# A recurrence and a two-layer network on one core: two transposes by TensorE instead of DMA, in a new order of steps

## The chip, the core and the metric

The kernel runs on one core of a Trainium2 chip. TensorE (PE) multiplies matrices into PSUM; VectorE (DVE), ScalarE (ACT) and GpSimd (POOL) do the element-wise work; SyncE (SP) issues nearly all DMA transfers from one queue. The metric is the device time of one execution in microseconds (us); the figure for a kernel is the median of its runs.

## The reference, cut to what matters

```python
# r, k, v, w: (4 batches, 8 heads, 768 steps, 48); u: (8, 48)
for t in range(768):
    cur = einsum('bhd,bhe->bhde', u * k_t, v_t)
    y[:, :, t] = einsum('bhd,bhde->bhe', r_t, state + cur)
    state = w_t[..., None] * state + einsum('bhd,bhe->bhde', k_t, v_t)
x = y.transpose(0, 2, 1, 3).reshape(3072, 384)
h = x @ w_in                       # (384, 2048)
out = maximum(0.01 * h, h) @ w_out # (2048, 384)
```

The first half is a linear recurrence over time for each batch and head; the second half takes its result y as rows and sends them through two matrix products with a leaky ReLU in between.

## The kernel before, in words

**Tiles.** The 768 steps of a batch are cut into 6 chunks of 128, so there are 24 chunks, numbered 0 to 23 in the order in which they are worked on (the "9th" is chunk 8, the "11th" chunk 10). Chunks 0 to 3 are done in pairs by `pair` (from L537), the others one at a time by `single` (from L741). The network works on blocks of one or two chunks: 15 blocks with 2, 1, 1, 1, 1, 2, 2, 2, 2, 2, 1, 1, 2, 2, 2 chunks.

**One chunk in `single`.** Four DMA loads w, k, r, v, 192 KB each (L755), into one of 10 buffers `in`. ACT takes the logarithm of w (`lw`, L765). PE sums it over time (the step `cum`, L771 and L774), DVE adds `lw` (`ci`, L783), ACT takes exponentials (L797, L801, and the decays `a`, L792), DVE multiplies them with r and k (`rk`, L459). `rk` is transposed to `rkT`, either by PE (L470) with a copy out of PSUM (L475 on DVE, L477 on ACT) or, for the chunks in `RK_DMA`, by a DMA transpose on SP (L818). PE multiplies `rkT` with itself (`scores`, L912, for some pairs of chunks in one step), DVE masks the result (`m`, two operations, L842). `sums` (L852) is the state's new part and DVE adds the old one (L867) that POOL has decayed (`sb`, L829). `intra` (L878 and L883) gives the chunk's product; DVE adds the bonus part to it (`y`, L532), which POOL and DVE prepared (L489, L493, L497, L501).

**From y to the network.** y has to be transposed into `xT`. For a chunk not in `Y_DMA`, `to_xt` does it: three transposes on PE (L518) into the PSUM bank that held the product, then one copy by ACT (L525) or DVE (L523). For a chunk in `Y_DMA`, SP issues one DMA transpose (L897).

**The network.** For each block, `up` steps (L1074) multiply `w_in` with `xT`, ACT applies the leaky ReLU (`g`, L1089), `down` steps (L1104, four for each chunk) multiply `g` with `w_out`; the result is copied out of PSUM (L1115 on DVE, L1117 on ACT) and stored by SP (L1121). The last three blocks of two chunks use a product scheme with seven instead of eight parts (L1006 on PE, with L989, L1020, L1022 and L1027 on DVE and ACT).

**The order.** Nothing runs in the order in which it is written. Each step is entered in a `Plan` with its engines, a duration, a priority and what it depends on. `Plan.order` goes through a list schedule: whenever an engine is free, it takes the ready step with the lowest priority that finds its buffers free. The table `RANK` adds a number to the priority of single steps, and `FORCE` fixes the engine of some that may run on two. The order that comes out is emitted, engine by engine, and on the chip each engine works through its own list strictly in that order, waiting on semaphores. SP's list holds all loads, stores and DMA transposes. There are 8 PSUM banks; at most two are given to `up` results (`hp`) and two to the products of `sums` and `intra` (`yy`).

Of the kernel before, what the change touches and what calls it, by code (L numbers as in the profile page):

```python
# [23 lines left out]
class Plan:  # L24
# [202 lines left out]
FORCE = {23: "DVE", 26: "DVE", 29: "ACT", 30: "DVE", 46: "ACT", 58: "ACT", 61: "ACT", 79: "ACT", 85: "DVE",  # L227
    112: "DVE", 114: "ACT", 117: "DVE", 119: "ACT", 121: "ACT", 123: "DVE", 125: "POOL", 127: "ACT", 128:
    "POOL", 134: "POOL", 137: "DVE", 139: "POOL", 142: "ACT", 143: "POOL", 492: "DVE", 500: "ACT", 604: "DVE",
    612: "ACT", 904: "DVE", 910: "DVE", 932: "ACT", 952: "ACT", 966: "ACT", 1002: "ACT", 1030: "ACT", 1075:  # L230
    "ACT", 1080: "ACT"}


@with_exitstack
def kernel(
# [23 lines left out]
    JQ = NJ // NQ  # L259

    RK_DMA = {6, 11, 12, 14, 15, 16, 17, 18, 19, 20, 21, 22, 23}
    Y_DMA = {8, 10, 16, 17, 20, 21, 22, 23}
    MERGED = {6, 10, 12, 14, 16, 18, 20}
    LEAD = 4
    AHEAD = 4
# [65 lines left out]
    with tc.manual_schedule():  # L331
# [180 lines left out]
        def to_xt(P0, y, yp, s_ye, col_of):  # L512
            def yT():
                return yp.t[:].bitcast(BF16).rearrange("p (g t) -> p g t", t=128)

            def typose(e):
                for g in range(KT):
                    nc.tensor.transpose(  # L518
                        yT()[:, g, :], y.t[:].rearrange("p h d -> p (h d)")[:, g * 128 : (g + 1) * 128], ident[:])

            def xcopy(e):
                if e == "DVE":
                    nc.vector.tensor_copy(out=col_of(), in_=yT()[:, 0:KT, :])  # L523
                else:
                    nc.scalar.copy(out=col_of(), in_=yT()[:, 0:KT, :])  # L525
            s_yt = step({"PE": 0.18}, typose, P0 + 1, deps=[s_ye], reads=[y, yp])
            return step({"ACT": 0.48, "DVE": 0.36}, xcopy, P0 + 1, deps=[s_yt], reads=[yp])
# [213 lines left out]
        def single(n):  # L741
# [149 lines left out]
            col = n * L  # L891
            if n not in Y_DMA:
                xt_steps[n] = [to_xt(P0, y, yp, s_ye, lambda: xT[:, :, col : col + L])]
# [287 lines left out]
```

## Time and profile before

| | |
|---|---|
| median of 3 runs | 180.65 us (180.39 to 180.79) |
| profiled execution | 181.35 us, span 179.6 us |
| granted TensorE clock | 1.000 |
| busy PE / DVE / ACT / POOL | 172.6 / 132.2 / 115.7 / 104.0 us |
| DMA | 34.43 MB in 116715 packets |
| y transposes by DMA (L897) | 8, of 1.23 us on SP (median), 3.5 us to landing |
| y transposes by PE (L518) | 48 matmuls, 219 ns each |

The span runs from the first to the last instruction of the profiled execution; its own time is 1.75 us longer and lies 0.70 us above the median of the runs. A line of a group gives line, engine, operation, out<-in, shapes and count, then busy time and mean duration in ns, then the idle time of the engine just before and what ended it. A line of a stage gives its bounds, its length, then busy time and count for PE, weight loads, DVE, ACT and POOL, the granted clock, the DMA share and GB/s. A line of the timeline or of the chain gives its start and length in us. Matmuls follow one another in a pipeline, so a step's share of PE is read from the start of the next step and not from the duration of its matmuls.

### The profile page before, as it was taken

What the parts mean: (1) busy time and instruction counts of PE and PEld (TensorE: products, weight loads), DVE (VectorE), ACT (ScalarE), POOL (GpSimd) and SP (SyncE); (2) the same over time, 40 slices, a digit from 0 to 9 for tenths busy, and PEclk for the clock granted to TensorE, in tenths of its full rate; (3) what the DMA queues carried; (4) which work ended last, traced back from release to release, by engine and by line L of the source; (5) the groups of instructions that cost most, each with busy time, mean ns of one, the idle gap of its engine ahead of it and who ended that gap; (6) DMA issues with size and microseconds to landing.
All of it is one profiled execution on the core that took longest, in us unless ns stands there. A gap on an engine that the chain in (4) does not pass through costs nothing.

```text
span 179.6 us, 5374 instructions
## 1 busy us (share of the span) xinstructions
PE 172.6 (96%) x2109; PEld 135.2 (75%) x2109; DVE 132.2 (74%) x265; ACT 115.7 (64%) x257; POOL 104.0 (58%) x138
## 2 busy tenths in 40 slices
PE   7998999999999999999999999999999999999991
PEld 2475878867878687787688777677778798899991
DVE  7589974189788898559687659499787599777472
ACT  2568968865957786895379775177675487735620
POOL 5989631675896486878468855414995459200000
PEclk9999999999999999999999999999999999999999
DMA  5999999999999989999899999999599996613004
GB/s 139 261 283 314 370 380 362 176 203 208 215 195 202 192 192 150 183 199 182 193 214 177 218 164 214 212 192 144 117 201 145 198 234 170 153 24 115 0 22 153
DMA packets 116715, 34.43 MB, mean 192 GB/s; under 512 B 109137, under 2 KB 115922, under 8 KB 116690
## 3 DMA queue, kind: packets, MB, share of 16 engines
q1 hardware_dynamic: 116688, 34.09, 90.8%
q8 instruction: 16, 0.26, 0.6%
q14 instruction: 9, 0.07, 0.1%
q10 hardware_dynamic: 2, 0.00, 0.0%
HBM read 25.17 MB, written 4.72 MB: 166 GB/s over the span
## 4 chain that ended last, share of the span: by engine, by line
PE 64%; DVE 8%; DMA 8%; ACT 6%; issue 5%; SPq 4%; POOL 3%; DVEq 0%; ACTq 0%; POOLq 0%
PE ps L1074 26%; PE ps L1104 17%; PE ps L1006 6%; DMA in<-in_w_dram 6%; SPq L755 3%; PE ps L1146 3%; PE ps L912 2%; DMA xT<-y 2%; DVE m L842 2%; POOL ru L489 1%; DVE o L1027 1%; ACT g L1089 1%; PE ps L883 1%; ACT rkT L477 1%; DVE m L690 1%
## 5 line engine op out<-in xcount | busy, mean ns | idle before, releaser
L1074 PE MATMUL ps<-xT,w_in_b 128*128 128x256 bf16 (+1 forms) x720 | 73.1, 251 | 0.4 <-ACT xT L525 0.2
L1089 ACT ACTIVATE g<-ps 128x512 bf16<-128x512 f32 x96 | 56.4, 595 | 20.6 <-PE ps L1074 15.3
L1074 PEld LDWEIGHTS <-w_in_b 128*128 128x128 bf16 x720 | 57.7, 98 | 9.3 <-issue 0.7
L1104 PE MATMUL ps<-w_out_b,g 128*128 128x384 bf16 x288 | 56.0, 326 | 0.1
L1104 PEld LDWEIGHTS <-g 128*128 128x128 bf16 x288 | 25.7, 97 | 12.4 <-ACT g L1089 0.2
L489 POOL TENSOR_TENSOR ru<-in,ub 128x384 f32<-128x384 f32 x24 | 24.5, 1027 | 10.9 <-DMA in<-in_k_dram 10.1
L459 DVE TENSOR_TENSOR rk<-in,ps 128x384 bf16<-128x384 f32 x46 | 24.3, 548 | 7.8 <-ACT ps L797 4.2
L842 DVE TENSOR_TENSOR m<-ps,maskb 128x512 bf16<-128x512 f32 x40 | 25.4, 683 | 6.1 <-PE ps L912 5.0
L493 POOL TENSOR_TENSOR ru<-ru,in 128x384 f32<-128x384 f32 x24 | 24.6, 1030 | 2.9 <-DMA in<-in_r_dram 2.2
L829 POOL TENSOR_TENSOR sb<-s,a 128x384 bf16<-128x384 f32 x18 | 15.7, 873 | 9.5 <-ACT a L792 9.4
L501 POOL TENSOR_TENSOR vs<-in,dg 128x384 f32<-128x384 f32 x20 | 16.6, 828 | 7.1 <-DVE dg L497 4.7
L509 POOL CAST vb<-in 128x384 bf16<-128x384 f32 x24 | 12.0, 503 | 11.3 <-DMA in<-in_v_dram 7.5
L783 DVE TENSOR_TENSOR ci<-ps,lw 128x384 f32<-128x384 f32 x20 | 11.1, 554 | 4.3 <-PE ps L771 1.9
L497 DVE TENSOR_REDUCE dg<-ru 128x8 f32<-128x384 f32 x24 | 12.9, 545 | 1.0 <-POOL ru L493 0.8
L765 ACT ACTIVATE lw<-in 128x384 bf16<-128x384 f32 x20 | 10.4, 520 | 3.6 <-DMA in<-in_w_dram 3.6
L797 ACT ACTIVATE ps<-ps 128x384 f32<-128x384 f32 x20 | 9.5, 475 | 4.2 <-DVE ci L783 3.8
L532 DVE TENSOR_TENSOR y<-ps,vs 128x384 bf16<-128x384 f32 x20 | 11.1, 553 | 1.5 <-PE ps L883 0.6
L867 DVE TENSOR_TENSOR s<-ps,sb 128x384 f32<-128x384 f32 x14 | 7.7, 552 | 4.0 <-PE ps L852 2.8
L801 ACT ACTIVATE ps<-ci 128x384 f32<-128x384 f32 x20 | 9.8, 488 | 0.6 <-DVE ci L783 0.6
L1146 PE MATMUL ps<-zeros 128*128 128x128 bf16 (+1 forms) x40 | 8.7, 339 | 1.3 <-DVE zeros L332 1.3
L525 ACT COPY xT<-ps 128x384 bf16<-128x384 bf16 x11 | 5.2, 481 | 6.8 <-PE ps L518 6.7
L792 ACT ACTIVATE a<-ps 64x4 f32<-64x4 f32 x36 | 6.0, 168 | 5.3 <-DVE ci L783 3.5
(105 smaller groups left out, 228.7 us busy)
## 6 DMA issues: line engine op xcount, KB each, us to landing
out_dram<-o SPq DMA_DIRECT2D x23, 192.0 KB, 3.2
in<-in_w_dram SPq DMA_DIRECT2D x20, 192.0 KB, 4.3
in<-in_k_dram SPq DMA_DIRECT2D x20, 192.0 KB, 4.2
in<-in_r_dram SPq DMA_DIRECT2D x20, 192.0 KB, 4.1
in<-in_v_dram SPq DMA_DIRECT2D x20, 192.0 KB, 4.3
in<-in_moe_w_out_dram SPq DMA_DIRECT2D x4, 768.0 KB, 12.3
in<-in_moe_w_in_dram SPq DMA_DIRECT2D x4, 384.0 KB, 7.0
in<-in_moe_w_in_dram SPq DMA_DIRECT2D x2, 768.0 KB, 9.8
```

Source lines behind the costliest of these rows:

```text
L459: (nc.gpsimd if e == "POOL" else nc.vector).tensor_tensor(out=o, in0=x, in1=i, op=ALU.mult)
L489: lambda e: nc.gpsimd.tensor_tensor(out=ru.t[:], in0=kv(), in1=ubv, op=ALU.mult),
L493: lambda e: nc.gpsimd.tensor_tensor(out=ru.t[:], in0=ru.t[:], in1=rv(), op=ALU.mult),
L497: lambda e: nc.vector.tensor_reduce(out=dg.t[:], in_=ru.t[:], axis=AX.X, op=ALU.add),
L501: lambda e: nc.gpsimd.tensor_tensor(out=vs.t[:], in0=vv(), in1=dg.t[:].unsqueeze(2).to_broadcast([128, H, D]), op=ALU.mult),
L509: {"POOL": 0.56}, lambda e: nc.gpsimd.tensor_copy(out=vb.t[:], in_=vv()),
L829: lambda e: nc.gpsimd.tensor_tensor(out=sb.t[:].rearrange("p g a d -> p (g a) d"), in0=s_in.t[:].rearrange("p g a d -> p (g a) d"), in1=a_ ...
L842: lambda e, par=par: nc.vector.tensor_tensor(out=m.t[:, par, :, :], in0=sc[par].t[:].rearrange("p (g t) -> p g t", g=NP), in1=maskb[:].uns ...
L1074: nc.tensor.matmul(hp.t[:, a * N : (a + 1) * N], lhsT=w_in_b[:, t, (j + a) * 128 : (j + a + 1) * 128], rhs=xT[:, t, c0 : c0 + N], start=(a ...
L1089: lambda e, hp=hp, g=g, j=j, J=J, N=N: nc.scalar.activation(out=g.t[:, j : j + J, 0:N], in_=hp.t[:, 0 : J * N].rearrange("p (a n) -> p a n ...
L1104: nc.tensor.matmul(op.t[:, 0:DM], lhsT=g.t[:, j, off : off + 128], rhs=w_out_b[:, j, :], start=(j == 0), stop=(j == NJ - 1))
L1146: nc.tensor.matmul(warm.t[:, 0:n], lhsT=zeros[:, 0:128], rhs=zeros[:, 0:n], start=True, stop=True, skip_group_check=True)
```

## The change

Chunks 8 and 10 leave `Y_DMA`: their y goes through `to_xt`, three transposes on PE and one copy, where it was one DMA transpose on SP. Two steps become four, so all later steps have other numbers. `RANK` and `FORCE` have new entries for nearly every step from number 165 on, where before they had entries from 491 to 715 and from 901 on; the entries up to 143 are the same.

```diff
-    143: -47.83, 491: 891.86, 492: -139.67, 493: -7.6, 494: -7.59, 497: 881.86, 498: -149.67, 499: 881.58,
...
+    143: -47.83, 165: 36.67, 166: -197.45, 169: 1035.44, 170: 17.7, 171: 1050.69, 172: -2.61, 178: 0.32, 180:
+    -233.6, 181: -249.28, 182: -249.28, 183: -20.34, 184: 8.39, 185: 1034.73, 186: -61.74, 187: 1138.21, 188:
...
-    "POOL", 134: "POOL", 137: "DVE", 139: "POOL", 142: "ACT", 143: "POOL", 492: "DVE", 500: "ACT", 604: "DVE",
-    612: "ACT", 904: "DVE", 910: "DVE", 932: "ACT", 952: "ACT", 966: "ACT", 1002: "ACT", 1030: "ACT", 1075:
-    "ACT", 1080: "ACT"}
+    "POOL", 134: "POOL", 137: "DVE", 139: "POOL", 142: "ACT", 143: "POOL", 172: "DVE", 186: "ACT", 188: "ACT",
+    201: "ACT", 239: "DVE", 253: "DVE", 261: "ACT", 277: "DVE", 279: "ACT", 311: "ACT", 325: "DVE", 341:
...
     RK_DMA = {6, 11, 12, 14, 15, 16, 17, 18, 19, 20, 21, 22, 23}
-    Y_DMA = {8, 10, 16, 17, 20, 21, 22, 23}
+    Y_DMA = {16, 17, 20, 21, 22, 23}
```

What the new entries make of the lists: PE's is the same up to the start at 41.58 us of the trace, DVE's to 40.21, SP's to 41.46, ACT's to 43.45 and POOL's to 45.00; behind that all five differ. PE has 2115 matmuls instead of 2109, SP 142 transfers instead of 144. DVE has two more copies to `xT`; one state copy, one output copy and one half copy of the last blocks go from DVE to ACT. The last eleven steps of PE are the same.

More of the change, by code (lines that the diff above doesn't have):

```diff
@@ L178 @@
     -65.55, 135: -2.69, 136: -61.05, 137: -65.8, 138: -2.37, 139: -61.55, 140: -57.81, 141: -2.69, 142: -64.8,
[48 rows of a table removed]
[109 rows of a table added]
 FORCE = {23: "DVE", 26: "DVE", 29: "ACT", 30: "DVE", 46: "ACT", 58: "ACT", 61: "ACT", 79: "ACT", 85: "DVE",
     112: "DVE", 114: "ACT", 117: "DVE", 119: "ACT", 121: "ACT", 123: "DVE", 125: "POOL", 127: "ACT", 128:
-    "POOL", 134: "POOL", 137: "DVE", 139: "POOL", 142: "ACT", 143: "POOL", 492: "DVE", 500: "ACT", 604: "DVE",
-    612: "ACT", 904: "DVE", 910: "DVE", 932: "ACT", 952: "ACT", 966: "ACT", 1002: "ACT", 1030: "ACT", 1075:
-    "ACT", 1080: "ACT"}
+    "POOL", 134: "POOL", 137: "DVE", 139: "POOL", 142: "ACT", 143: "POOL", 172: "DVE", 186: "ACT", 188: "ACT",
+    201: "ACT", 239: "DVE", 253: "DVE", 261: "ACT", 277: "DVE", 279: "ACT", 311: "ACT", 325: "DVE", 341:
+    "DVE", 343: "DVE", 421: "ACT", 423: "DVE", 445: "DVE", 502: "ACT", 772: "ACT", 786: "ACT", 822: "ACT",
+    850: "ACT", 878: "ACT", 906: "ACT", 912: "DVE", 934: "DVE", 940: "DVE", 954: "ACT", 996: "ACT", 999:
+    "DVE", 1004: "ACT", 1040: "ACT", 1074: "ACT", 1082: "ACT"}
 @with_exitstack
```

154 rows, old and new, of the table RANK are left out of this document.

## The prediction

> **What bounds the kernel now.** I read the page's busy times first, then its chain, then the busy time by stage, and last the timeline wherever the chain leaves TensorE (PE).
>
> ```profile
> PE 172.6 (96%) x2109; PEld 135.2 (75%) x2109; DVE 132.2 (74%) x265; ACT 115.7 (64%) x257; POOL 104.0 (58%) x138
> L1104 PE MATMUL ps<-w_out_b,g 128*128 128x384 bf16 x288 | 56.0, 326 | 0.1
> L518 PE MATMUL ps<-ident,y 128*128 128x128 bf16 x48 | 5.1, 219 | 0.0
> 60.00:70.00 10.00, 9.79 (x128) 7.83 (x127) 9.27 (x19) 7.42 (x18) 7.57 (x10) 1.00 0.87 176
> 90.00:100.00 10.00, 10.00 (x116) 8.38 (x114) 7.76 (x16) 8.53 (x21) 7.69 (x10) 1.00 1.05 203
> ```
>
> PE has nearly no gap: in most stages from 30 us on it is busy 10.00 us of 10.00, at the full granted clock (1.00). The row at 60 is one of the two worst there: 0.21 us idle, with DVE at 9.27. So the order of steps can give back only what PE waits for. I took that from the starts of neighbouring steps (a step that waits for nothing begins 0.65 us after a `down` began, 0.66 after an `up`, 0.17 after a y transpose). From 40 us on four waits above 0.15 us stand in the part before 90 us:
>
> ```profile
> 47.92 4.93 DMA in<-in_w_dram
> 52.94 0.53 ACT lw L765
> 53.51 0.32 PE ps L771
> ...
> 65.24 5.14 DMA in<-in_w_dram
> 70.41 0.53 ACT lw L765
> 70.98 0.32 PE ps L771
> ...
> 85.77 3.72 DMA xT<-y
> 89.53 1.47 PE ps L1074 x12
> ```
>
> This is the chain of waits. The `w` loads of chunks 8 and 11 land late, so `cum` starts at 53.51 and 70.98; the steps before it began at 53.06 and 70.36 and are worth 0.17 us each, so PE lost 0.28 and 0.45. The y of chunk 10, moved by DMA, lands just before 89.53; the 16 `scores` matmuls before it began at 88.80 and take 0.55, so 0.18 lost. The fourth is no transfer:
>
> ```profile
> 61.42 0.82 PE L1104 MATMUL ps<-w_out_b,g 128*128 128x384 bf16 x4
> 61.55 0.35 ACT L792 ACTIVATE a<-ps 64x4 f32<-64x4 f32 x2 [1.08 <-DVE ci L783]
> 61.92 0.48 ACT L525 COPY xT<-ps 128x384 bf16<-128x384 bf16 x1
> 62.45 0.81 PE L1074 MATMUL ps<-xT,w_in_b 128*128 128x256 bf16 x6 [0.20 <-ACT xT L525]
> ```
>
> `down` could have been followed at 62.07; the `up` began at 62.45: 0.38 lost, because the copy of xT stood behind two small ACT operations. After 90 us I find only 0.16, 0.22 and 0.20 and, in the last products (from 173 us), 0.65. All that an order could recover is thus about 1.3 us before 90 us, 0.6 after it and perhaps 0.6 at the end.
>
> **The change, part by part.**
>
> *Added on PE:* 2 chunks x 3 transposes (L518). From the timeline three of them hold PE 0.17 us (the row's 219 ns each overlap). 2 x 0.17 = +0.33 us. PE has no gap to take it, so all of it lies on the path.
>
> By the Trainium skill ("VectorE: DVE Perf Modes", section The three transpose paths) one 128x128 bf16 transpose costs 390 ns on TensorE; by that figure the six would be, as an estimate, +2.34 us in place of +0.33. The trace disagrees: 219 ns for one, 0.17 us for three in a row.
>
> *Added on DVE and ACT:* in the new order DVE makes two more copies to xT, 2 x 0.358 (L523), and ACT as many as before. One state copy (0.547, L865), one output copy (0.554, L1115) and one half copy (0.352, L1020) go from DVE to ACT, where they cost 0.49, 0.48 and 0.32. DVE nets -0.74 us, ACT +1.29. At 74% and 64% busy the rest of their time hides this; without that cover it would be up to +0.6. I take 0. The new transposes also keep the bank of the y product until the copy is done, one transpose and one copy longer (about 0.8 us with the turn); at most two such banks are given out, and the state product of a later chunk wants one. I take 0, since the new transposes stand only three to four steps behind `intra`, and keep 0.2 for the range.
>
> *Removed on SP:* two DMA transposes, 1.23 us each of SP's queue (median; 1.94 and 1.18 here) and 3.5 us to landing. Chunk 8's xT was used at 72.5 us, well after its 66.52 issue plus 3.5, so it gives nothing itself; chunk 10's gives back the 0.18. Behind them SP held the loads of r and v (68.50, 69.56 and 87.04, 87.94), none of which a PE wait leads back to.
>
> *Moved:* PE keeps its order to 41.58 us; after that the attention steps are spread differently and the `up` steps of a block come in another order. The work is the same. Three things follow.
>
> Loads. The `w` load of chunk 8 now stands ahead of r and v of chunk 7 and no longer behind an output store; the one of chunk 11 stands behind a load that waits only for the `cum` of chunk 9, not behind an output store; those of chunks 10, 13, 16 and 17 start with much more PE work between issue and use. I expect both waits gone: -0.28 -0.45 = -0.73. Bounds: 0 (the loads come as late as before) and -0.73. One load gets less room: `w` of chunk 14 now stands behind the store of chunk 8's result, and between the `down` that ends this result and `cum` of 14 lie 7.8 us of PE work. Needed are 0.7 for the copy, 0.65 to 1.0 for the store on SP, 4.9 to 5.1 from the load's issue to its landing and 0.6 for lw: 6.9 to 7.4. That is just enough: 0, up to +0.5 if the copy before the store is late.
>
> First turn. The first transposes of chunk 5 move up ahead of two `down` steps. By the rows: m starts at 40.21, then ci at 40.82, the other m at 41.28, the r product at about 41.93 (behind ACT's 0.47 from 41.41), ready at 42.5; PE, through `down`, `down` and `intra`, is there at 42.43. +0.1.
>
> Short turns. A result that leaves PE and comes back needs, at the shortest in this trace, 0.81 us for y (0.20 to DVE, 0.55, 0.06 back), 0.65 or 0.73 for a copy to xT, and about 0.8 for g. I counted the PE work that each order leaves in between, with the step times above. Before, four turns have less than 0.3 us to spare (the y and the copy of chunk 18, one g, one lw); in the new order seventeen: the y of chunks 5, 6, 7, 10, 12, 14, 18 and 19, the copies of 5, 9, 15 and 19, and five g. (For chunk 5, `intra` to y transpose: before, a `cum` 0.26, an `up` 0.66, a `sums` 0.17 and a `down` 0.65, 1.74 us; now a `down` and a `sums`, 0.82.) DVE and ACT do other things in between, and what one of these steps loses is not caught up, as PE has no gaps. Bounds for the 13 more: the four of before cost together 0.1, so +0.3; or each costs what the copy at 61.92 cost, 0.38, so +4.9. I take one in five at 0.38: 13 x 0.076 = +1.0, nearer to the low end because three of the four cost nothing.
>
> Sum: +0.33 -0.18 -0.73 +0.1 +1.0 = +0.5 us. The profiled execution took 181.35 us: a span of 179.6 and 1.75 around it; it lies 0.70 above the median of the runs, 180.65. So a profile of the changed kernel should show a span near 180.1, and the runs 180.65 + 0.5, about **181.2 us**.
>
> **The rivals.**
>
> *Faster: the short turns hold.* Then the loads, xT of chunk 10 and the copy at 61.92 give back 0.73 + 0.18 + 0.38 = 1.29, and the new cost is 0.33 + 0.1: -0.86, 179.8 us. For it: three of the four tight turns of before cost nothing, and the stage from 90 to 120 us shows that PE can run without a gap. Against it: seventeen such turns, six of them between 40 and 70 us, where DVE is 85 to 93% busy. It decides below one turn in fifteen at 0.38.
>
> *No change.* About half of the turns' price, +0.5: the sum is 0, 180.65 us.
>
> *Much slower: SP stalls behind a store.* If the copy ahead of the store before the `w` load of chunk 14 comes late, `cum` of 14 waits, and the paired `scores` of 14 and 15, with DVE's work for both, slip with it. It decides from 0.7 us late on; from there each us is lost. At 1.7 late: +0.5 +1.0, 182.2 us. Against it: SP's longest wait at a store (L1121) is 1.1 us, and no late load in the trace costs PE over 0.45.
>
> *The dear transpose.* 390 ns each would give +0.5 +2.0, 183.2 us. The 48 transposes of this trace measure it, so I give it under 1 in 100. That is the skill page named above; the trace does not bear it out.
>
> *It does not do what it says.* PE gets the transposes but xT of chunk 10 is no sooner used: the gain of 0.18 is missing, 181.3 us; within the forecast.
>
> **How the numbers follow.** About 0.2% (0.36 us) is what can be told from no change here. Slower by more: 0.42 for the forecast's case (own range 181.0 to 182.0) and 0.10 for SP's stall, 0.52. Faster by more: 0.30. Between: 0.18. The range goes from 179.7 (all of the faster case, and a little of the 0.2 after 90 us) to 182.6 (the forecast's case with twice the turns' price, or SP's stall at 2 us); one in ten is left out at each end, the dear turns at +4.9 among them.
>
> **What would show it.** In the profile after: `cum` after 53 and 70 us without a wait for lw (right) or with one (the loads' step wrong); no DMA on the chain between `intra` of chunk 10 and its `up`; L518 with 54 matmuls at 219 ns; new waits of PE on DVE's y and ACT's g between 45 and 75 us (the short turns), or PE at 10.00 of 10 there, which would prove the forecast wrong and the faster case right. A PE wait above 0.5 us at `cum` of chunk 14 would be SP's stall.

## The result, and the profile after

The changed kernel takes **182.53 us** (median of four runs, 181.96 to 182.91) against 180.72 for the kernel before beside it: a ratio of 1.0099, 95% interval 1.0081 to 1.0118, or +1.8 us. Run again it took 182.32 against 180.57, 1.0086 (1.0058 to 1.0115), or +1.55 (a ratio is taken from all the runs and need not be the quotient of the medians, which here is 1.0097). The sign and the range of the prediction hold; the point, 181.2, lay 1.1 to 1.3 us too low.

In the profile after, lines of the code behind the tables have numbers higher by 63 (L518 is now L581, L1074 is L1137, L771 is L834). First the page of the changed kernel, with busy time and share of each engine, the chain's shares, and the `down` matmuls:

```profile
PE 172.4 (96%) x2114; PEld 134.9 (75%) x2115; DVE 130.7 (73%) x264; ACT 117.0 (65%) x260; POOL 104.1 (58%) x138
...
PE 77%; DVE 6%; ACT 6%; DMA 3%; SPq 3%; issue 2%; DVEq 0%; ACTq 0%
...
L1167 PE MATMUL ps<-w_out_b,g 128*128 128x384 bf16 x288 | 56.3, 326 | 0.0
```

Before, the chain was 64% PE and 8% DMA:

```profile
PE 64%; DVE 8%; DMA 8%; ACT 6%; issue 5%; SPq 4%; POOL 3%; DVEq 0%; ACTq 0%; POOLq 0%
```

Now it is 77% PE and 3% DMA. The transfers that PE waited for between 50 and 90 us are gone, and the kernel is still slower. The stages show where PE now stands still (the columns are those of the stages before):

```profile
60.00:70.00 10.00, 10.00 (x133) 8.03 (x131) 7.78 (x16) 8.23 (x19) 6.28 (x8) 1.00 1.15 186
90.00:100.00 10.00, 9.78 (x118) 7.40 (x117) 7.31 (x15) 6.14 (x16) 6.02 (x9) 1.00 1.15 208
100.00:110.00 10.00, 9.77 (x84) 7.12 (x81) 5.68 (x11) 8.61 (x23) 8.43 (x12) 1.00 0.94 174
```

The stage from 60 to 70 us, one of the two worst before, is full. The one from 90 to 100 us, full before, has lost 0.22, and the next one, which was full too, 0.23. That one before:

```profile
100.00:110.00 10.00, 10.00 (x103) 7.41 (x102) 6.44 (x13) 7.26 (x18) 6.69 (x9) 1.00 1.18 188
```

The clock is 1.00 in all.

The timeline of the changed kernel names these waits. In brackets stand the idle time before an instruction and what ended it:

```profile
45.95 0.59 ACT L540 COPY rkT<-ps 128x512 bf16<-128x512 bf16 x1
46.59 0.40 PE L975 MATMUL ps<-rkT 48*128 48x128 bf16 x8 [0.26 <-ACT rkT L540]
...
72.31 0.35 DVE L586 COPY xT<-ps 128x384 bf16<-128x384 bf16 x1
72.71 0.49 PE L1137 MATMUL ps<-xT,w_in_b 128*128 128x256 bf16 x3 [0.18 <-DVE xT L586]
...
98.09 0.55 DVE L595 TENSOR_TENSOR y<-ps,vs 128x384 bf16<-128x384 f32 x1
98.70 0.34 PE L581 MATMUL ps<-ident,y 128*128 128x128 bf16 x3 [0.22 <-DVE y L595]
...
102.13 0.94 ACT L828 ACTIVATE lw<-in 128x384 bf16<-128x384 f32 x2
102.70 0.32 PE L834 MATMUL ps<-lw,trev 128*128 128x384 bf16 x1 [0.23 <-ACT lw L828]
```

Each pair is one short turn: a result leaves PE, another engine works on it, and PE stands ready before it is back. The bracket counts from the end of the matmul before, which overlaps the next one; from the starts of the steps, as in the prediction, PE loses 0.42, 0.32, 0.36 and 0.40 us at these four (0.1 of the first is a fixed part that stands ahead of every `scores` step, before the change too). The second and third were named as short turns beforehand; the copy to rkT of chunk 5 and `lw` of chunk 17 were not.

The end differs too. The kernel before:

```profile
175.53 0.82 PE L1006 MATMUL ps<-w_out_b,in 128*128 128x192 bf16 x8 [0.32 <-DVE o L1027]
...
176.39 0.36 DVE L1027 TENSOR_TENSOR o<-ps,o 128x192 f32<-128x192 f32 x1 [0.65 <-PE ps L1006]
```

And the changed kernel:

```profile
175.50 0.82 PE L1069 MATMUL ps<-w_out_b,in 128*128 128x192 bf16 x8
176.41 0.89 DVE L1090 TENSOR_TENSOR o<-ps,o 128x192 f32<-128x192 f32 x3 [1.02 <-PE ps L1069]
```

Before, PE waits 0.48 us ahead of its last product for an addition that reads the same bank (c22 in the code), and one addition follows the last matmul. After, that addition stands behind the product, PE does not wait, and three additions follow. From the end of the last matmul to the end of the span it is 3.29 us before and 3.93 after.

**How runs are compared here.** PE's list is the same in both kernels up to 41 us, but the time it takes to get there is not the same in every execution: the first transposes of chunk 4 start at 38.42 us in the profile of before and at 37.90 in that of after. So from each profile I take the *stretch*, from that start to the end of the span (by the traces' own stamps 179.640 - 38.416 = 141.22 and 180.248 - 37.904 = 142.34 us; the pages give a span to 0.1 us only), beside the sum of PE's waits behind 40 us (start of the next step less start of this one and its standard length; some 1 us of it in the fixed 0.1 us at each `scores`) and the time behind the last matmul.

| kernel | median, us | ratio to before (95%) | stretch | PE waits | behind last matmul |
|---|---|---|---|---|---|
| before, two profiles | 180.65; 180.73 (one run) | | 141.22; 141.14 | 4.01; 3.88 | 3.29; 3.33 |
| after, two profiles | 182.53; 182.32 | 1.0099; 1.0086 | 142.34; 142.35 | 4.15; 4.15 | 3.93; 3.93 |
| old_order_pe | 180.85 | 1.0007 (0.9988 to 1.0026) | 141.52 | 4.01 | 3.24 |
| new_order_no_tr | 182.29 | 1.0087 (1.0058 to 1.0116) | 142.14 | 4.29 | 3.93 |
| new_order_filled | 182.16 | 1.0087 (1.0050 to 1.0125) | 141.80 | 3.59 | 3.95 |
| old_order_loads | 181.08 | 1.0000 (0.9978 to 1.0021) | 140.64 | 3.43 | 3.29 |
| old_order_filled | 181.06 | 1.0007 (0.9986 to 1.0028) | 141.36 | 4.13 | 3.29 |
| old_order_filled_pe | 181.32 | 1.0020 (1.0004 to 1.0037) | 141.22 | 3.68 | 3.28 |
| new_order_end | 182.39 | 1.0065 (1.0043 to 1.0087) | 142.31 | 4.72 | 3.34 |
| new_order_filled_end | 182.36 | 1.0055 (1.0034 to 1.0075) | 142.20 | 4.62 | 3.32 |
| old_order_copy_end | 181.82 | 1.0010 (0.9981 to 1.0038) | 141.31 | 3.42 | 3.96 |
| new_order_late | 181.41 | 1.0049 (1.0032 to 1.0067) | 141.59 | 3.63 | 3.70 |

One of the twelve runs of old_order_copy_end (183.58 us) was in a slower state and counts in its median but not in its ratio; without it the median is 181.68.

The runs were made on different chips, on which the kernel before had medians of 180.57, 181.01, 181.56 and 180.42 us, so kernels from different chips are compared by their ratios alone. Stretch by stretch the change costs 142.35 - 141.18 = 1.17 us: 0.33 for the transposes, about 0.2 more of PE waits, and 0.6 behind the last matmul. The timed ratios say 1.8 and 1.55; the interval of the second, 1.05 to 2.08 us, holds 1.17, that of the first, 1.46 to 2.13, does not. The difference of 0.4 to 0.6 us I can't place: the timed runs give a span and a clock but no stages.

### The profile page after: what moved, and what is told of

Same layout as the page of the kernel before. It is cut to its first block, busy times and chain, and to the rows that moved or that the text cites. A ratio compares the mean times of both kernels' runs of the same rounds, so it can differ in the third digit from the quotient of the medians.

```text
span 180.2 us, 5386 instructions
## 1 busy us (share of the span) xinstructions
PE 172.4 (96%) x2114; PEld 134.9 (75%) x2115; DVE 130.7 (73%) x264; ACT 117.0 (65%) x260; POOL 104.1 (58%) x138
## 3 DMA queue, kind: packets, MB, share of 16 engines
HBM read 25.17 MB, written 4.72 MB: 166 GB/s over the span
## 4 chain that ended last, share of the span: by engine, by line
PE 77%; DVE 6%; ACT 6%; DMA 3%; SPq 3%; issue 2%; DVEq 0%; ACTq 0%
PE ps L1137 33%; PE ps L1167 22%; PE ps L1069 7%; DMA in<-in_k_dram 3%; PE ps L975 3%; SPq L607 3%; PE ps L533 2%; PE ps L946 2%; DVE ci L846 2%; PE ps L834 2%; PE ps L581 1%; PE ps L941 1%; PE ps L915 1%; DVE m L753 1%; ACT ps L860 1%
## 5 line engine op out<-in xcount | busy, mean ns | idle before, releaser
L1137 PE MATMUL ps<-xT,w_in_b 128*128 128x256 bf16 (+1 forms) x720 | 73.5, 251 | 0.3 <-DVE xT L586 0.2
L1137 PEld LDWEIGHTS <-w_in_b 128*128 128x128 bf16 x720 | 57.4, 98 | 8.6 <-issue 0.7
L552 POOL TENSOR_TENSOR ru<-in,ub 128x384 f32<-128x384 f32 x24 | 23.8, 1001 | 12.7 <-DMA in<-in_k_dram 12.7
L564 POOL TENSOR_TENSOR vs<-in,dg 128x384 f32<-128x384 f32 x20 | 17.6, 881 | 4.9 <-DVE dg L560 3.2
L572 POOL CAST vb<-in 128x384 bf16<-128x384 f32 x24 | 12.7, 533 | 10.6 <-DMA in<-in_v_dram 8.3
L1209 PE MATMUL ps<-zeros 128*128 128x128 bf16 (+1 forms) x39 | 8.0, 321 | 1.3 <-DVE zeros L395 1.3
```

Of the source, the lines that this page charges most:

```text
L552: lambda e: nc.gpsimd.tensor_tensor(out=ru.t[:], in0=kv(), in1=ubv, op=ALU.mult),
L564: lambda e: nc.gpsimd.tensor_tensor(out=vs.t[:], in0=vv(), in1=dg.t[:].unsqueeze(2).to_broadcast([128, H, D]), op=ALU.mult),
L572: {"POOL": 0.56}, lambda e: nc.gpsimd.tensor_copy(out=vb.t[:], in_=vv()),
L1137: nc.tensor.matmul(hp.t[:, a * N : (a + 1) * N], lhsT=w_in_b[:, t, (j + a) * 128 : (j + a + 1) * 128], rhs=xT[:, t, c0 : c0 + N], start=(a ...
```

## The experiments

**The two kernels once more.** No edit. 

> The changed kernel unaltered, for a second profile and a closer time. Theory A (the change's cost lies in waits of TensorE that the new order makes, and the profiled execution of after, the shortest of its four runs, was a lucky one in its first 20 us): 182.0 to 182.9 us, a span above 180.2, and the waits behind 40 us at the same steps and of the same size: scores of chunk 5 0.42, up of block 6 0.32, y transposes of chunk 12 0.36, cum of chunk 17 0.40, last up of block 12 0.24. Rival B (profile against profile, +0.6 us, is the true difference): about 181.3 us.

> The kernel before unaltered, for a second profile. Its 21 runs so far lie between 180.08 and 181.68 us while the profiled execution that the prediction was worked from took 181.35. Theory A (that execution was an unlucky one, and the waits of cum on the w loads of chunks 8 and 11, 0.28 and 0.45 us, are smaller in most): a span of 178.4 to 179.1 and together less than 0.4 us of these waits. Rival B (the waits are the same in every execution): both within 0.05 us of 0.28 and 0.45.

Theory A held for the changed kernel's waits, not for its being caught at a lucky moment: the span is again 180.2, and every wait behind 40 us is the same to 0.007 us. Two of them in the second profile:

```profile
98.69 0.34 PE L581 MATMUL ps<-ident,y 128*128 128x128 bf16 x3 [0.22 <-DVE y L595]
...
102.69 0.32 PE L834 MATMUL ps<-lw,trev 128*128 128x384 bf16 x1 [0.23 <-ACT lw L828]
```

The kernel before is not so steady. Its second profile (timeline of PE):

```profile
53.24 0.32 PE L771 MATMUL ps<-lw,trev 128*128 128x384 bf16 x1 [0.28 <-ACT lw L765]
...
70.25 0.33 PE L771 MATMUL ps<-lw,trev 128*128 128x384 bf16 x1
...
88.88 0.38 PE L1074 MATMUL ps<-xT,w_in_b 128*128 128x256 bf16 x2 [0.25 <-DMA xT<-y]
```

`cum` of chunk 8 now loses 0.44 (0.28 in the first profile), `cum` of 11 nothing (0.46), and the `up` behind the y of chunk 10 loses 0.32 (0.18). Together 0.76 against 0.92. The span, 179.0, is as theory A has it, the waits are neither theory's: both executions lose 0.8 to 0.9 us at these three places, but not at the same ones.

**The old order, transposes on PE (old_order_pe).** The DMA transposes of chunks 8 and 10 are left out of SP's list, and the transposes and copies of `to_xt` are put into free banks. Steps 292 and 375 are the DMA transposes; `turn_y` emits three transposes of a chunk into the bank named, `copy_y` its copy on the engine named (cuts marked):

```diff
+        ahead_of = {814: lambda: turn_y(8, 7), 356: lambda: copy_y(8, 7, "DVE"), 382: lambda: turn_y(10, 3), 383: lambda: copy_y(10, 3, "ACT")}
...
         for i in order:
+            if i in (292, 375):
+                continue
+            if i in ahead_of:
+                ahead_of[i]()
```

> The kernel before with its order of steps kept; only the y of chunks 8 and 10 is transposed on TensorE in place of the two DMA transposes, three matmuls each put ahead of the last up of block 5 and of the y transposes of chunk 11, with the copies on VectorE and ScalarE. Theory A (the order of steps is what costs): the six transposes 2 x 0.17, less the wait of 0.18 us on the xT of chunk 10: +0.15, so 0 to +0.4 us over before. Rival B (the transposes themselves, their copies and the banks they hold are what costs): +1.3 to +1.8 us over before.

Measured 1.0007, that is +0.13 us (-0.2 to +0.5); the stretch is 0.34 longer. This is theory A. That the stretch fits so well is in part chance, since in this execution `cum` of chunk 7 lost 0.70 us and `cum` of 11 nothing. Three transposes in the timeline of this kernel, then three that it had before, each set taking PE 0.17 us:

```profile
85.80 0.33 PE L1144 MATMUL ps<-ident,y 128*128 128x128 bf16 x3
85.97 0.33 PE L518 MATMUL ps<-ident,y 128*128 128x128 bf16 x3
86.14 0.81 PE L1107 MATMUL ps<-w_out_b,g 128*128 128x384 bf16 x4
```

**The new order without the transposes (new_order_no_tr).**

```diff
         def to_xt(P0, y, yp, s_ye, col_of):
...
             def typose(e):
-                for g in range(KT):
+                for g in range(0 if P0 in (80, 100) else KT):
```

> The changed kernel and its order, with the six y transposes of chunks 8 and 10 left out; the two copies remain and bring numbers of the y product, of the same size, into xT in their place. Theory A (the order costs): only the transposes' own 2 x 0.17 us are gone, 0.1 to 0.6 us below the changed kernel. Rival B (the transposes cost): 1.3 to 1.8 us below it, back to the kernel before.

The six matmuls are left out, so the network's rows for these two chunks are not the right ones. The copies and all else stay. 1.0087 against 1.0086: nothing came back that the runs show, not even the 0.1 of theory A's lower edge. In the stretch, 0.20 of the 0.33 did; PE's waits are 0.14 longer, with a new one of 0.20 us ahead of the rkT transposes of chunk 13. Rival B is out from this side too. The cost is the order.

**The new order with its waits filled (new_order_filled).** Steps of PE that were ready are emitted earlier; the same three lines, with other pairs, make all moves below.

```diff
+        for x, ahead in [(774, 193), (820, 834), (877, 436), (881, 529), (953, 984)]:
+            order.remove(x)
+            order.insert(order.index(ahead), x)
```

> The changed kernel with five of TensorE's steps moved ahead of the five steps at which its profile shows TensorE waiting: an up of block 3 ahead of scores of chunk 5, a down of block 5 ahead of the first up of block 6, two downs of block 7 ahead of the y transposes of chunk 12 and of cum of chunk 17, a down of block 10 ahead of the last up of block 12. No other engine's order changes. Theory A (these waits are the cost): 0.42 + 0.32 + 0.36 + 0.40 + 0.24 = 1.7 us less at most, so 1.2 to 1.7 us below the changed kernel, near 181.0 us. Rival B (a wait filled here comes back at the next step, or the cost is not in these waits): within 0.4 us of the changed kernel.

1.0087, no gain that the runs show; the stretch is 0.54 shorter. All five waits are gone and others stand in their place: 0.26 at the rkT transposes of chunk 7, 0.30 at the y transposes of chunk 10, 0.25 at the first `up` of block 8, 0.31 at `sums` of chunk 18. Two of them in the timeline, the first before PE's weight load:

```profile
52.52 0.23 PEld L533 LDWEIGHTS <-rk 128*128 128x128 bf16 x4 [0.47 <-DVE rk L522]
...
85.32 0.34 PE L581 MATMUL ps<-ident,y 128*128 128x128 bf16 x3 [0.16 <-DVE y L595]
```

This is rival B for some two thirds of the 1.74, by the profile: PE reaches the next step earlier, and that one's input comes no sooner.

**The old order with its waits filled.** First the two load waits alone:

```diff
+        for x, ahead in [(783, 268), (814, 354)]:
```

> The kernel before with two of TensorE's steps moved: the last down of block 3 ahead of cum of chunk 8 and the last up of block 5 ahead of cum of chunk 11, so that the two late w loads are covered. Theory A (the 0.73 us of load waits that the prediction gave back are in only a part of the executions): 0 to 0.4 us faster than before. Rival B (they are in all): 0.5 to 0.75 us faster.

1.0000: theory A by time. The profiled stretch is 0.54 shorter, which is what rival B asked, but it is one execution. Then five waits, on PE and ACT:

```diff
+        for x, ahead in [(261, 301), (783, 268), (814, 354), (852, 856), (946, 619)]:
```

> The kernel before with its five largest waits between 50 and 135 us covered: besides the two steps ahead of cum of chunks 8 and 11, a down of block 6 ahead of the first up of block 7, an up of block 10 ahead of cum of chunk 20, and on ScalarE the xT copy of chunk 7 ahead of the two small operations for chunk 9. Theory A (what a filled wait gives stays given): 0.28 + 0.45 + 0.18 + 0.38 + 0.38 = 1.7 us at most, 1.2 to 1.6 us faster than before. Rival B (a third is kept, as in the changed kernel, where 1.74 us of filled waits shortened the stretch from 40 us to the last matmul by 0.57): 0.4 to 0.7 us faster.

1.0007 (-0.25 to +0.5 us): neither theory; no gain shows. The timeline shows how a filled wait returns:

```profile
52.95 0.52 ACT L765 ACTIVATE lw<-in 128x384 bf16<-128x384 f32 x1 [1.85 <-DMA in<-in_w_dram]
...
53.67 0.33 PE L771 MATMUL ps<-lw,trev 128*128 128x384 bf16 x1
...
54.53 0.62 PE L912 MATMUL ps<-rkT 48*128 48x128 bf16 x16 [0.45 <-DMA rkT<-rk]
...
70.86 1.00 POOL L489 TENSOR_TENSOR ru<-in,ub 128x384 f32<-128x384 f32 x1 [1.59 <-DMA in<-in_k_dram]
...
74.33 0.51 POOL L509 CAST vb<-in 128x384 bf16<-128x384 f32 x1
...
74.89 0.29 PE L852 MATMUL ps<-vb,rk 128*128 128x96 bf16 x3 [0.37 <-POOL vb L509]
```

`cum` of chunk 8 (53.67) starts without a wait for the late load, and the next step, `scores` of chunk 6, waits for a DMA transpose of rkT instead, 0.59 us from the starts; at 74.89 `sums` of chunk 11 waits for POOL's copy of v. That copy is the fifth POOL operation in a row without a gap, and the first of the five, at 70.86, had waited 1.59 us for chunk 11's k load. PE was early; a transfer and POOL's list behind another were not.

> The same as the run with the five waits of the kernel before covered, and the y of chunks 8 and 10 transposed on TensorE. Theory A (the transposes cost their own 2 x 0.17 us and nothing else): 0.2 to 0.4 us slower than that run. Rival B (they take a bank, a copy or a slot in a queue that the order has no room for): over 0.6 us slower than it.

1.0020 against 1.0007: +0.23 us, theory A, though the two intervals overlap and the stretch, 0.13 shorter, does not show it. A third measurement that puts the six transposes at their own time or less.

**The end.**

```diff
+        for x, ahead in [(1083, 1084)]:      # c22 ahead of the last product
```

> The changed kernel with one VectorE step of the last block moved: the addition that makes c22 ahead of the last product on TensorE, as in the kernel before. In the changed kernel it stands behind that product and waits for it, because both use one bank, and three additions (0.89 us) follow the last matmul in place of one (0.36). Theory A (the end is a part of the cost): the last product starts about 0.2 us later, behind it stands one addition and no longer three with their two stores, 0.3 to 0.55 us faster than the changed kernel. Rival B (what the end wins TensorE loses ahead of the last product, 0.48 us in the kernel before): within 0.15 us of the changed kernel.

The stretch is 142.31, within 0.04 of the changed kernel's. Behind the last matmul 0.60 were won, and PE waits 0.42 more ahead of the last product; a new wait of 0.15 in block 13 took the rest:

```profile
176.86 0.82 PE L1069 MATMUL ps<-w_out_b,in 128*128 128x192 bf16 x8 [0.25 <-DVE o L1090]
...
177.71 0.36 DVE L1090 TENSOR_TENSOR o<-ps,o 128x192 f32<-128x192 f32 x1 [0.65 <-PE ps L1069]
```

By the profile this is rival B. By time it is open: the ratio, 1.0065, is 0.4 to 0.6 us better than the changed kernel's two, which is what theory A asked, but the intervals overlap.

> The changed kernel with both corrections: the five filled waits and the c22 addition ahead of the last product. Theory A (the new order costs through its turns and its end, and both add up): 0.57 from the stretch behind 40 us and 0.45 at the end, 0.8 to 1.2 us faster than the changed kernel, 181.1 to 181.6 us. Rival B (the filled waits come back elsewhere, as the timed runs of that kernel alone say): only what the end gives, 0.3 to 0.55.

1.0055, -0.56 us against 1.0086 with overlapping intervals and -0.8 against 1.0099, clear of it; the stretch is the changed kernel's less 0.14. Theory A is at best at its lower edge: in this execution the rkT transposes of chunk 7 alone waited 0.78, behind an r load for which DVE had stood still 1.05 us.

> The kernel before with two moves that no transfer has a part in: on ScalarE the xT copy of chunk 7 ahead of the two small operations for chunk 9, and on VectorE the c22 addition behind the last product and behind the c21 addition. Theory A (waits on other engines are the same in every execution, so covering them pays): 0.38 for the up behind the copy and, at the end, 0.48 that TensorE no longer waits less 0.3 for a second addition behind the last matmul, together 0.3 to 0.6 us faster than before. Rival B (the freed time is waited for at a later step): within 0.15 us of before.

1.0010 and a stretch 0.13 longer: rival B. The `up` behind the copy of chunk 7 no longer waits and PE loses nothing ahead of the last product, so its waits are 0.5 to 0.6 smaller; the additional addition and store behind the last matmul cost 0.63 to 0.67 (3.96). The end costs the same in either form, within some 0.2 us.

**Only behind 95 us (new_order_late).** The last run asks where the new order loses, since by bins of 10 us its waits up to 90 us and the transposes are no more than the waits of before.

```diff
+        for x, ahead in [(877, 436), (880, 886), (881, 529), (953, 984), (1080, 1083)]:
```

> The changed kernel with moves behind 95 us only: three downs of block 7 ahead of the y transposes of chunk 12, the first up of block 8 and cum of chunk 17, a down of block 10 ahead of the last up of block 12, and at the end the c21 addition ahead of the c22 addition, both still behind the last product's start. Nothing before 95 us is touched. Theory A (the new order loses its time behind 90 us, where its waits are 2.65 us against 2.06 in the profile of before, and in three additions behind the last matmul): 0.36 + 0.40 + 0.24 of waits and 0.27 at the end, of which a fourth may come back: 0.8 to 1.3 us faster than the changed kernel, a ratio to before of 1.001 to 1.005. Rival B (waits filled here come back in full at later steps): 0 to 0.4 us faster, a ratio above 1.006.

1.0049: 0.65 to 0.9 us faster than the changed kernel by the ratios, and 0.76 shorter in the stretch, the only correction of the new order that both show (its interval lies clear of the changed kernel's first one and overlaps the second by little). Stage from 90 to 110 us of this kernel:

```profile
90.00:100.00 10.00, 10.00 (x121) 7.55 (x119) 7.30 (x15) 6.08 (x14) 6.36 (x8) 1.00 1.09 209
100.00:110.00 10.00, 10.00 (x93) 7.35 (x92) 5.64 (x11) 9.07 (x25) 8.62 (x12) 1.00 0.85 165
```

PE is full again where the changed kernel had 9.78 and 9.77. This is theory A, at its lower edge: by the two measures 0.65 to 0.9 of the 1.27 us that was covered stayed won. It is still slower than the kernel before, and no kernel of these beats that.

## Why the prediction was right or wrong, point by point

The direction was right; the size, +0.5 against +1.55 to +1.8, was not. That the time lies inside the range is owed to the range's margin: the two cases that the prediction names for its upper end come, by its own terms, to 180.65 + 1.5 = 182.15 and 180.65 + 1.8 = 182.45, not to 182.6, and neither came about. The span foretold for the profile, near 180.1, was met (180.2) by luck, since the profile of after went through its first 38 us 0.51 us faster than the profile of before.

**Transposes, +0.33: right.** The group of the changed kernel:

```profile
L581 PE MATMUL ps<-ident,y x54: 216/219/230, 17.0 to 139.8; 128*128 128x128 bf16 x54
```

The 54 matmuls at 219 ns are there, and by time six of them cost +0.13 (old_order_pe), +0.23 (old_order_filled_pe) and, left out, nothing measurable. By the Trainium skill ("VectorE: DVE Perf Modes", section The three transpose paths), 390 ns each would be, as an estimate, +2.34 us; the interval of old_order_pe ends at +0.5, so the measurement decides against it.

**The DMA transpose of chunk 10, -0.18: right as a wait.** No DMA stands between `intra` of 10 and its `up`, which starts at 86.26 without a wait.

**The loads, -0.73: the step that was mis-sized.** As forecast no `cum` waits after 53 and 70 us. But the term took a wait that disappears for time that is won. Covering the same two waits in the old order moved the time by 0.0 us (-0.4 to +0.4), and the profiles show other steps waiting in their place: `sums` of chunk 11 in old_order_loads (0.34), that and `scores` of chunk 6 in old_order_filled (0.53 and 0.59). How much returns in this way is not settled, as the one profile of old_order_loads kept 0.54. Also their size was read from one execution, and in another it was 0.44 and 0. With 0 in place of -0.73 the sum is +1.25, or 181.9.

**SP's stall at chunk 14: did not come.** `lw` of 14 was done at 98.03 and `cum` started at 98.08. "Just enough" was the right reading, with nothing to spare.

**First turn, +0.1: right**, 0.09 in both profiles.

**Short turns, +1.0: the size was near, the list was not.** Of the named ones four cost something: y of 5 (0.06), xT of 9 (0.32), y of 12 (0.36), y of 18 (0.10, as before), 0.84 in all; none of the five g did (the g that cost is another). Outside the list came the rkT copy of 5 (0.42), `lw` of 17 (0.40), `scores` of 18 and 19, held halfway (0.24), the last `up` of block 12, behind ACT's g (0.24), and a product of the last block, behind a DVE addition (0.36): 1.66, or 1.56 without the 0.1 that `scores` of 5 lost before too. So the term's size is in part a coincidence. Against that, waits of before that the sum had not counted are gone too: the copy at 61.92 (0.38) and four others (0.72). I had counted turns of y, xT and g only; the turns over rkT, `lw` and banks are as short. And I looked for them between 45 and 75 us, where DVE is busiest, while the only cost that a run took away again lay behind 95 (new_order_late).

**The end: missing from the sum.** I took the last eleven steps of PE for unchanged, which they are, but DVE's are not: 0.64 more behind the last matmul, 0.48 less ahead of it, +0.16. The prediction read 0.65 us of PE's waits in the last products; the rows give 0.48. The 0.65 in the rows of before shown above is DVE's idle time ahead of its last addition.

Term by term by the profiles: 0.33 - 0.18 - 0.73 + 0.09 + 0.74 + 1.56 - 0.38 - 0.72 + 0.16 = +0.87, against 1.12 between the same two profiles; the rest is spread over differences below 0.06 at single steps. The total of +0.5 was then too low by 0.4 to 0.7 in the terms, and by the 0.4 to 0.6 that stays open.

**DVE and ACT, 0: no cost shown.** DVE went from 132.2 (131.2 in the second profile) to 130.7, ACT from 115.7 (116.0) to 117.0, about as counted. **The bank held longer, 0:** no wait behind the new transposes leads to it.

## What to carry to other kernels

Where an engine is 96% busy and fed by three others and a queue of transfers, its waits can't be added up as gains: a wait that goes can return in part or in whole at the next step whose input is no earlier, so price a removed wait by what is late next; of the waits covered here between nothing and some two thirds stayed won. Compare such kernels from a common step onward, since the same first steps took 37.8 to 38.7 us in the profiles here, and look at the whole of the last block, where an addition that moves behind the last product cost about as much as the wait it saved. When an order is suspected, keep it and change the operation, then keep the operation and change the order: two runs settled that here.

## What the runs showed of the hardware

The waits of the changed kernel, none of which its profile puts down to a transfer, repeated to 0.007 us from one execution to the next. Waits on transfers did not: in the profiles of the old order `cum` of chunk 7 lost 0, 0.07, 0.10, 0.48 and 0.70 us, and `cum` of 11 0.46 in one and nothing in the others that left it where it was. The same kernel before had medians from 180.42 to 181.56 us on four chips at a granted clock of 0.995 to 1.000, which is as large as most effects in this study.
